# A planner's clock that lets GpSimd's masks and VectorE's SBUF operations exclude each other, in a two-layer transformer kernel

## The chip, the core and the metric

The kernel runs on one core of a Trainium2 chip. The metric is the device time of one launch in microseconds. The engines are named as in the profile: PE (TensorE matmul, with PEld its weight loads), DVE (VectorE), ACT (ScalarE), POOL (GpSimd) and SP (SyncE, which here only issues DMAs).

## The reference

Two blocks are applied twice in turn to x, 2048 rows of 512 in bfloat16, with the same weights both times:

```python
x = x + A(layernorm(x));  x = x + B(layernorm(x))      # and the same two lines again

# A: 32 heads of 16 columns, four segments of 512 rows each
logits = q @ k.T / 4 + mask;  a_dot = softmax(logits) @ v      # causal within its segment, as 0 / -1e9 by row and column
a_mem  = (phi(q) @ M) / (phi(q) @ z + 1e-6)                    # phi(t) = t + 1 if t > 0 else exp(t)
o      = g * a_mem + (1 - g) * a_dot                           # g = sigmoid(beta), one per head
M += phi(k).T @ v;  z += sum(phi(k))                           # carried from segment to segment
A      = o @ wo

# B
B      = (gelu(x @ w_gate) * (x @ w_up)) @ w_down              # 512 -> 1792 -> 512, tanh form of gelu
```

## The kernel before

The work goes by eight segments: four of the first pass and four of the second, numbered k = 0 to 7, each of 512 rows. For each there is an `Att` object (block A) and an `Ffn` object (block B). All weights, x and the segment's intermediates stay in SBUF. The eight PSUM banks of 128x512 float32 are handed out one by one (`pick`), and a bank is free again when some engine has read it.

PE's work comes in three tilings. A dense product of 128x128x512 is issued whole (line 532) or in four column pieces of 32 (line 527). The scores (line 992) run as four row tiles of 32 rows, and the product of probabilities and values, called flush (line 1008), as four column tiles. Between tilings PE switches.

For a segment's attention there are 36 rounds of scores. Two rounds fill two pairs of banks, ACT takes the exponential of each pair into a `pt` slot (line 1434), POOL or DVE zeroes the part above the diagonal (the masks, lines 1381, 1386 and 1391), and a flush uses nine rounds or so. DVE then transposes the flush's result (byq, line 1025), divides (ab, line 1033) and transposes back (aT, line 1040). Between the rounds stand the dense products: q, k, v; the memory's products; wo; 14 gate products, 14 up products and four down products of 14 steps. Their results are taken out of PSUM by DVE or ACT (`evict`, lines 517 and 518), and added to x by DVE (line 1081). Layer norm is on DVE (statistics at line 570, xn at line 600, sometimes on POOL). The normalised rows are turned by DMA transposes on SP's queue, or by PE and an eviction for those that `by_pe` names (line 642).

Gate results are kept in `gel_sb`. When all kept gates of a segment are there, `gelu_all` sets ACT to Gelu alone (`act.only`), which also loads another activation table, and ACT applies Gelu in place (line 1195). The last `direct` gates, by their number, stay in PSUM and get their Gelu straight from there (line 1121). Segment 7 takes all its Gelus straight from PSUM (line 1108).

No engine chooses anything when the kernel runs. The order of every engine's instructions is made when the kernel is built, by the function `order`. It keeps a clock for PE and one for each other engine (`Clocks`, `Engine`). At each step it asks what PE can do now: two rounds of scores (`rounds_now`), the next piece of an open product, or the product with the least due time among those that are ready by the clocks. If nothing is ready and a bank is free, it issues a fill, a matmul on the constant tile `warm`. If no bank is free it lets the clock run. Each other engine takes from its posted jobs the one with the least ready time plus slack (`Engine.serve`). The costs are numbers in the code, in microseconds. Due times and slacks are in `POLICY`, and `CHANGES` replaces some of them in single stretches of 20 us of the planned time. Only the order reaches the chip. Semaphores keep it right, and where a cost is wrong an engine waits.

VectorE's and GpSimd's operations with all operands in SBUF have a cost of type `Slowed`: a time alone and an amount that is added if the other engine's last such operation is still running by the clock:

```python
if isinstance(cost, Slowed):
    if self.rival.port > t + 0.1:
        t += cost.more
    self.port = t + cost
```

The mask operations of POOL have plain costs.

Of the kernel before, what the change touches and what calls it, by code (L numbers as in the profile page):

```python
# [11 lines left out]
ACT = mybir.ActivationFunctionType  # L12
# [16 lines left out]
FT = FF // P  # L29
# [18 lines left out]
def round_of(t):  # L48

    b, i = divmod(t, ROUNDS)  # L50
    if i == SHARED:
# [18 lines left out]
    flush_wait=31.032, piece_slack=12.114, kb_slack=17.26, mem_slack=-3.651, margin=2.436, qk_due=1.242,  # L70
    e_q=-0.78, e_k=1.726, exp_slack=-22.194, e_slack=6.379, phi_slack=16.481, gelu_slack=5.207, act_evict=5.099,
    first_evict=-1.454, gate_step=0.008, up_due=0.23, up_step=0.048, down_due=1.972, down_step=0.411,
    upd_due=0.836, kb_act=0.601, vz_slack=0.631, x_dve=1.439, v0_due=-1.871, x1_at=-24.71, x2_at=15.224,
    x3_at=27.505, x3_load=5.352, direct=2, gelu_tiles=1, look=3.643, lag=0.5, wv_at=6.266, xn_pool=3.14,
    kb_pool=4.2, cut_pool=2.678, at_pool=8.009, pe_turns=1, early=5.887, starve=0.39, near=-4.229, cap=3,
    soon=5.328)

CHANGES = {
    1: dict(flush_wait=32.067, phi_slack=16.21, gelu_slack=7.718, up_due=0.251, upd_due=0.421, x_dve=2.027,
        look=2.465, early=5.04),  # L80
    2: dict(flush_wait=32.067, phi_slack=16.21, gelu_slack=7.718, up_due=0.251, upd_due=0.471, x_dve=2.027,
        look=2.465, early=5.04),
    3: dict(flush_wait=29.115, piece_slack=3.287, kb_slack=20.041, mem_slack=-6.163, qk_due=1.326, e_q=-0.807,
        e_k=1.562, exp_slack=-23.374, phi_slack=17.368, gelu_slack=4.829, act_evict=3.476, first_evict=-1.146,
        up_due=0.102, up_step=0.03, down_due=1.953, down_step=0.413, upd_due=0.93, vz_slack=-1.163, look=4.182,
        xn_pool=4.557, kb_pool=4.735, cut_pool=0.095, at_pool=7.177, early=5.489, near=-2.667, cap=2, soon=4.536),
    4: dict(mem_slack=-5.18, margin=3.412, qk_due=1.158, exp_slack=-22.515, phi_slack=17.182, act_evict=5.723,
        down_due=2.119, vz_slack=0.498, look=3.219, xn_pool=4.585, cut_pool=3.546, at_pool=7.441, early=5.429,
        starve=0.478, soon=4.482),
    5: dict(kb_slack=15.09, mem_slack=-4.972, up_due=0.1, xn_pool=4.868, cut_pool=2.362),  # L90
    6: dict(mem_slack=-3.758, e_q=-0.911, e_k=1.815, act_evict=5.646, first_evict=-0.527, up_due=0.239,
        up_step=0.043, down_step=0.406, x_dve=1.274, direct=3, near=-5.575, cap=4),
    7: dict(flush_wait=27.914, mem_slack=-4.892, phi_slack=16.815, first_evict=-0.749, up_step=0.056, down_due=1.835,
        upd_due=0.824, kb_act=0.94, direct=1, lag=0.762, xn_pool=4.45, kb_pool=4.061, at_pool=7.125, early=5.542,
        starve=0.714, near=-4.302, cap=1, soon=3.714),
    9: dict(e_k=1.639, gelu_slack=5.187, up_due=0.23, up_step=0.05, kb_act=0.938, vz_slack=0.404, lag=0.612,
        kb_pool=3.937, cut_pool=3.32, early=5.784, cap=2, soon=5.439),
    10: dict(gelu_slack=5.187, up_due=0.23, upd_due=0.987, vz_slack=0.513, xn_pool=1.446, cut_pool=3.402,
        early=5.784, cap=2, soon=5.439),
    11: dict(gelu_slack=5.908, upd_due=0.987, vz_slack=0.513, xn_pool=1.446, cut_pool=3.402, early=5.784, cap=2,  # L100
        soon=5.439),
    12: dict(flush_wait=29.115, piece_slack=10.134, mem_slack=-4.176, margin=2.501, qk_due=1.047, e_k=1.581,
        e_slack=6.526, phi_slack=18.977, act_evict=5.661, first_evict=-0.966, gate_step=0.028, up_due=0.211,
        up_step=0.052, down_due=1.811, down_step=0.409, kb_act=3.137, x_dve=1.793, direct=1, look=2.233,
        cut_pool=2.844, early=5.595, cap=2, soon=4.119),
    13: dict(flush_wait=31.998, kb_slack=15.76, margin=2.188, qk_due=1.37, e_q=-0.681, e_k=1.607, exp_slack=-22.955,
        e_slack=8.005, phi_slack=17.246, gelu_slack=5.065, act_evict=6.326, first_evict=0.369, up_due=0.23,
        up_step=0.053, down_due=1.971, down_step=0.42, upd_due=0.833, kb_act=2.813, vz_slack=0.028, x_dve=1.225,
        direct=0, look=4.789, lag=0.833, xn_pool=1.003, kb_pool=6.227, cut_pool=1.872, early=4.965, starve=0.244,
        near=-4.281, soon=4.486),  # L110
    15: dict(flush_wait=29.717, piece_slack=13.149, kb_slack=19.294, mem_slack=-5.639, e_slack=6.767,
        first_evict=-0.318, up_due=0.26, up_step=0.056, down_due=2.016, kb_act=0.41, x_dve=1.289, look=2.582,
        cut_pool=4.981, at_pool=7.181, early=6.304),
    17: dict(flush_wait=30.781, piece_slack=8.881, kb_slack=18.357, mem_slack=-6.183, margin=2.678, qk_due=0.996,
        e_q=-0.614, e_k=1.779, exp_slack=-25.113, e_slack=8.371, phi_slack=17.054, gelu_slack=5.133, act_evict=5.437,
        gate_step=0.015, up_due=0.264, up_step=0.05, down_due=1.905, down_step=0.422, upd_due=0.6, kb_act=2.882,
        x_dve=2.377, gelu_tiles=3, look=2.018, lag=0.848, xn_pool=3.568, kb_pool=6.676, cut_pool=1.121,
        at_pool=7.491, early=5.072, near=-4.322, cap=5, soon=3.604),
    18: dict(flush_wait=34.707, piece_slack=8.536, kb_slack=18.053, mem_slack=-8.018, qk_due=1.188, e_q=-0.503,
        e_k=1.782, exp_slack=-23.593, e_slack=8.107, phi_slack=16.435, gelu_slack=5.168, act_evict=5.437,  # L120
        gate_step=0.007, up_step=0.045, down_due=2.315, upd_due=0.606, kb_act=1.877, vz_slack=-0.68, x_dve=1.741,
        gelu_tiles=2, look=2.51, lag=0.848, xn_pool=3.185, kb_pool=7.295, cut_pool=2.272, at_pool=6.929, early=5.072,
        near=-4.303, soon=3.604),
    20: dict(flush_wait=30.024, piece_slack=18.892, mem_slack=-5.208, qk_due=1.306, e_k=1.855, exp_slack=-24.126,
        e_slack=6.869, act_evict=6.671, first_evict=-1.8, gate_step=0.016, up_due=0.267, up_step=0.049,
        down_step=0.388, kb_act=1.799, vz_slack=-0.793, lag=1.151, kb_pool=3.298, cut_pool=2.948, at_pool=7.79,
        early=5.114, near=-5.599, soon=4.272),
    21: dict(flush_wait=28.52, piece_slack=18.892, mem_slack=-5.208, qk_due=1.306, e_q=-0.843, e_k=1.855,
        exp_slack=-24.126, e_slack=6.869, act_evict=6.671, first_evict=-1.8, gate_step=0.016, up_due=0.267,
        up_step=0.049, down_step=0.388, kb_act=1.799, vz_slack=-0.793, look=3.436, lag=1.151, kb_pool=3.298,  # L130
        cut_pool=2.948, at_pool=7.303, early=5.114, near=-5.599, soon=4.272),
    22: dict(flush_wait=30.024, piece_slack=18.892, mem_slack=-5.208, qk_due=1.306, e_q=-0.843, e_k=1.855,
        exp_slack=-24.126, e_slack=6.869, act_evict=6.671, first_evict=-1.8, gate_step=0.016, up_due=0.267,
        up_step=0.049, down_step=0.388, kb_act=1.799, vz_slack=-0.793, lag=1.151, kb_pool=3.298, cut_pool=2.948,
        at_pool=7.303, early=5.114, near=-5.599, soon=4.272),
    24: dict(kb_slack=19.342, mem_slack=-5.116, margin=2.033, e_slack=6.341, first_evict=-0.532, up_due=0.155,
        up_step=0.043, upd_due=0.729, vz_slack=0.073, look=4.821, lag=-0.099, at_pool=7.008),
    26: dict(kb_slack=19.342, mem_slack=-5.116, margin=2.033, e_slack=6.341, first_evict=-0.359, up_due=0.155,
        upd_due=0.729, kb_act=1.494, lag=-0.099, xn_pool=4.611, cut_pool=3.497, at_pool=7.008, cap=4),
    27: dict(kb_slack=19.342, mem_slack=-5.116, margin=2.033, e_slack=6.341, first_evict=-0.359, up_due=0.155,  # L140
        upd_due=0.729, kb_act=1.494, lag=-0.099, xn_pool=4.611, cut_pool=3.497, at_pool=7.008, cap=4),
}
WINDOW = 20.0


class Slowed(float):


    def __new__(cls, alone, more):
        self = super().__new__(cls, alone)  # L150
        self.more = more
        return self


class Engine:
# [4 lines left out]
    def __init__(self, overlap=0.0):  # L160
        self.free, self.overlap, self.jobs, self.table = 0.0, overlap, [], "exp"
        self.only, self.rival, self.port = None, None, 0.0
# [1399 lines left out]
```

## Time and profile before

| | us |
|---|---|
| median of 3 runs | 555.3 (553.71 to 556.18) |
| the profiled execution | 553.62 |
| its span, first to last instruction | 551.9 |
| PE busy | 536.3 (97%) |
| DVE busy | 463.3 (84%) |
| ACT busy | 428.2 (78%) |
| POOL busy | 304.2 (55%) |

In the profile a group of instructions is a line of the kernel, an engine, an operation, the tiles (out<-in), the shapes and a count. Behind the bar stand its busy time and the mean of one in nanoseconds, and behind the second bar the engine's idle time just before them and who ended it. A row of the timeline is a start, a length, an engine and a line, where like instructions that follow each other are merged into one row. Matmuls are pipelined, so one shows a longer time than the step from it to the next. A row of a stretch is its window and length, and PE's busy time with the number of instructions, its granted clock, and what DMA did. A row of the waits is who waited, for whom, microseconds in total, how many times, and the longest.

### The profile page before, as it was taken

The numbers are of one execution on the slowest core, as the hardware profiler recorded it, in microseconds if no ns is written. First come the engines' busy times: TensorE is split into PE (matmuls) and PEld (weight loads), VectorE is DVE, ScalarE is ACT, GpSimd is POOL, SyncE is SP. The second block draws the span as 40 slices with busy tenths as digits, with TensorE's granted clock in tenths as the row PEclk, the third lists the DMA queues.
The fourth block names the chain that finished last, engine by engine and source line by source line (L and its number), as shares of the span: only waits on it lengthen the run. The fifth ranks groups of instructions, "written<-read, shape, count | busy, mean of one in ns | idle before, by whom it ended". The sixth has DMA issues, their size and how long they took to land.

```text
span 551.9 us, 23372 instructions
## 1 busy us (share of the span) xinstructions
PE 536.3 (97%) x10286; PEld 279.5 (51%) x10286; DVE 463.3 (84%) x854; ACT 428.2 (78%) x557; POOL 304.2 (55%) x359
## 2 busy tenths in 40 slices
PE   7999999999999999999999989999999999999997
PEld 3454565554455454544554445554565556555544
DVE  6999999899998999879999897999779687876332
ACT  5899999987898978989899874898978977650330
POOL 2798889286763886336783372846867255200000
PEclk9999999999999999999999999999999999999999
DMA  8147401630140123310223031211222004100001
GB/s 248 42 96 194 140 20 24 163 47 7 32 78 12 23 41 61 59 23 3 40 40 61 2 42 23 50 34 31 51 51 51 2 13 89 23 2 21 20 1 38
DMA packets 67109, 27.59 MB, mean 50 GB/s; under 512 B 51392, under 2 KB 67008, under 8 KB 67008
## 3 DMA queue, kind: packets, MB, share of 16 engines
q1 hardware_dynamic: 66576, 25.84, 22.0%
q8 instruction: 80, 1.31, 1.0%
q10 hardware_dynamic: 432, 0.27, 0.2%
q14 instruction: 21, 0.17, 0.1%
HBM read 9.71 MB, written 2.10 MB: 21 GB/s over the span
## 4 chain that ended last, share of the span: by engine, by line
PE 73%; DVE 17%; issue 3%; ACT 2%; POOL 2%; DMA 2%; SPq 0%; DVEq 0%; ACTq 0%; POOLq 0%
PE ps L527 32%; PE ps L532 28%; PE ps L992 6%; PE ps L1008 5%; DVE st L570 2%; DVE x_sb L1081 2%; DVE xn L600 2%; DVE byq L1025 2%; ACT pt L1434 2%; DMA x_sb<-in_A_x_dram 2%; DVE phiq L799 1%; DVE kx L473 1%; DVE ab L1033 1%; POOL kx L473 1%; PE ps L642 1%
## 5 line engine op out<-in xcount | busy, mean ns | idle before, releaser
L1434 ACT ACTIVATE pt<-ps 128x1024 bf16<-128x1024 f32 x288 | 278.8, 1027 | 54.8 <-PE ps L992 47.3
L1381 POOL TENSOR_SCALAR_AFFINE_SELECT pt<-pt 128x256 bf16<-128x256 bf16 (+1 forms) x192 | 108.3, 579 | 102.9 <-ACT pt L1434 98.9
L1143 DVE TENSOR_TENSOR gel_sb<-gel_sb,ps 128x512 bf16<-128x512 bf16 x112 | 74.2, 683 | 28.4 <-PE ps L532 21.0
L1386 POOL TENSOR_SCALAR_AFFINE_SELECT pt<-pt 64x1024 bf16<-64x1024 bf16 x46 | 56.2, 1222 | 24.7 <-ACT pt L1434 20.0
L1081 DVE TENSOR_TENSOR x_sb<-x_sb,ps 128x512 bf16<-128x512 bf16 (+1 forms) x68 | 42.9, 645 | 26.6 <-PE ps L532 13.9
L527 PE MATMUL ps<-xnT,wu_sb 128*32 128x512 bf16 x1072 | 59.8, 379 | 0.0
L527 PE MATMUL ps<-wd_sb,gel_sb 128*32 128x512 bf16 (+1 forms) x1012 | 56.6, 367 | 0.2 <-DVE x_sb L1081 0.2
L818 POOL TENSOR_SCALAR e<-e 128x512 bf16<-128x512 bf16 x36 | 56.1, 1560 | 0.9
L527 PE MATMUL ps<-xnT,wg_sb 128*32 128x512 bf16 x924 | 55.6, 380 | 0.7 <-DVE gel_sb L517 0.6
L532 PE MATMUL ps<-xnT,wg_sb 128*128 128x512 bf16 x217 | 51.7, 380 | 0.3 <-DVE x_sb L1081 0.2
L532 PE MATMUL ps<-wd_sb,gel_sb 128*128 128x512 bf16 (+1 forms) x251 | 49.6, 345 | 0.8 <-DVE byq L1025 0.8
L1025 DVE STREAM_TRANSPOSE byq<-ps 128x512 f32<-128x512 f32 x64 | 44.5, 700 | 6.7 <-PE ps L1008 6.6
L1195 ACT ACTIVATE gel_sb<-gel_sb 128x512 bf16<-128x512 bf16 (+1 forms) x77 | 44.6, 668 | 0.1
L527 PEld LDWEIGHTS <-wu_sb 128*32 128x32 bf16 x1072 | 28.8, 97 | 27.1 <-issue 0.6
L532 PE MATMUL ps<-xnT,wu_sb 128*128 128x512 bf16 x180 | 41.7, 380 | 0.0
L570 DVE BATCH_NORM_STATS2 st<-x_sb 128x6 f32<-128x512 bf16 x60 | 40.6, 676 | 1.4 <-DMA x_sb<-in_A_x_dram 1.0
L517 DVE CAST gel_sb<-ps 128x512 bf16<-128x512 f32 x58 | 38.2, 679 | 2.9 <-PE ps L527 2.3
L527 PEld LDWEIGHTS <-gel_sb 128*32 128x32 bf16 x1012 | 25.6, 97 | 21.2 <-issue 1.8
L1008 PE MATMUL ps<-pt,vaug 128*32 128x256 bf16 (+2 forms) x1344 | 34.8, 238 | 0.0
L600 DVE TENSOR_SCALAR xn<-x_sb,mv,rs 128x512 bf16<-128x512 bf16 x57 | 32.8, 628 | 2.2 <-POOL rs L588 1.9
L527 PEld LDWEIGHTS <-wg_sb 128*32 128x32 bf16 x924 | 22.9, 97 | 21.3 <-issue 2.1
L532 PEld LDWEIGHTS <-gel_sb 128*128 128x128 bf16 x251 | 23.4, 98 | 19.7 <-issue 1.5
(146 smaller groups left out, 887.6 us busy)
## 6 DMA issues: line engine op xcount, KB each, us to landing
vz<-vaug SPq DMA_DIRECT2D x14, 136.0 KB, 2.6
wg_sb<-in_B_w_gate_dram SPq DMA_DIRECT2D x8, 224.0 KB, 4.4
wu_sb<-in_B_w_up_dram SPq DMA_DIRECT2D x8, 224.0 KB, 5.3
wd_sb<-in_B_w_down_dram SPq DMA_DIRECT2D x7, 256.0 KB, 5.5
x_sb<-in_A_x_dram SPq DMA_DIRECT2D x3, 512.0 KB, 7.6
out_dram<-x_sb SPq DMA_DIRECT2D x12, 128.0 KB, 1.8
xnT<-xn SPq DMA_TRANSPOSE x44, 2.5
wk_sb<-in_A_wk_dram SPq DMA_DIRECT2D x2, 256.0 KB, 6.5
```

What stands on the lines that cost most here:

```text
L527: nc.tensor.matmul(out[r], lhsT=lhsT[:, r], rhs=rhs, start=start, stop=stop, tile_position=(0, 32 * c))
L532: nc.tensor.matmul(out, lhsT=lhsT, rhs=rhs, start=start, stop=stop)
L570: nc.vector.bn_stats(out=self.st6[:, 0, :], in_=x_sb[:, self.tt0 + j, :])
L818: lambda eng: eng.tensor_scalar(out=e[0][:], in0=e[0][:], scalar1=1.0, scalar2=None, op0=ALU.min), summed)
L1008: nc.tensor.matmul(ps()[32 * j:32 * j + 32, q0:q0 + n], lhsT=va[:, ki * VW + g:ki * VW + g + 32], rhs=pt_all[:, places[i], j, c0:c0 + n], ...
L1025: nc.vector.transpose(out=self.byq[:, par, :, :].rearrange("p a c -> p (a c)"), in_=ps()[:])
L1081: ck.dve.post(ck.made(), slack, (0.15 + 0.00104 * (c1 - c0), lambda: nc.vector.tensor_tensor(out=xt, in0=xt, in1=ps()[:, 0:c1 - c0], op=AL ...
L1143: ck.dve.post(ck.made(), NORMAL, (0.683, lambda: nc.vector.tensor_tensor(out=g, in0=g, in1=ps()[:], op=ALU.mult), lambda t: (ps.read(t), e ...
L1195: return (0.205 + 0.427 * (f1 - f0), lambda: nc.scalar.activation(out=g, in_=g, func=ACT.Gelu_apprx_tanh), lambda t: self.gelu_done(t, f0, ...
L1381: nc.gpsimd.affine_select(out=view, in_=view, pattern=[[0, 4], [0, n], [1, C]], compare_op=ALU.is_ge, fill=0.0, base=C, channel_multiplier=-1)
L1386: nc.gpsimd.affine_select(out=view, in_=view, pattern=[[0, 4 * TPS], [1, C]], compare_op=ALU.is_ge, fill=0.0, base=0, channel_multiplier=-1)
L1434: nc.scalar.activation(out=pt_all[:, s0:s0 + 2, 2 * p:2 * p + 2, :].rearrange("p r h c -> p h r c"), in_=ps_all[:, pair[0]:pair[1] + 1, :] ...
```

## The change

The class `Slowed` becomes `Port`. A Port operation first waits, by the clock, until the other engine's hard Port operation ends, less 0.2 us. Operations of GpSimd on tensors with a scalar, and its addition to aT, are marked soft: they do not hold the other engine off, and the two cost 0.15 us if they meet. GpSimd's masks are hard Port operations now. Where a mask holds the port for more than 0.25 us longer, VectorE's Port jobs are put back by `shun` = 1.318 in the choice of the next job.

The Gelu stage is changed too. `direct` counts gates in the order in which they are done, not by number, and is 4 (2 before, and 0 to 3 in some stretches). Up to three neighbouring tiles go through one Gelu (one before, with few exceptions). The stage begins when no exponential is posted on ACT. While it lasts (`phase`) no new phi exponential starts, no new rounds of scores start while more than `hold` = 5 of the segment's 14 gates lack their Gelu, and the gates that are left are taken first.

The numbers of `POLICY` are new, `pe_turns` is 2 instead of 1 (the normalised rows of one more segment are turned by PE), and `CHANGES` is empty. The operations on data are the same in both kernels, but which engine does some of them, and the order on all engines, differ.

```diff
 POLICY = dict(
-    ..., x3_load=5.352, direct=2, gelu_tiles=1, look=3.643, ..., pe_turns=1, early=5.887, starve=0.39, ...)
+    ..., x3_load=17.807, direct=4, gelu_tiles=3, look=1.884, ..., pe_turns=2, gate_due=1.051, shun=1.318,
+    hold=5, early=5.58, starve=0.305, ...)
...
 CHANGES = {
-    1: dict(flush_wait=32.067, phi_slack=16.21, gelu_slack=7.718, up_due=0.251, upd_due=0.421, x_dve=2.027,
-        look=2.465, early=5.04),
...
 }
-class Slowed(float):
-    def __new__(cls, alone, more):
+class Port(float):
+    def __new__(cls, alone, soft=False):
         self = super().__new__(cls, alone)
-        self.more = more
+        self.soft = soft
         return self
...
-        job = min((j for j in jobs if j[0] + self.LATENCY <= start + 0.03), key=lambda j: j[0] + j[1])
+        held = self.rival is not None and self.rival.port > start + 0.25
+        job = min((j for j in jobs if j[0] + self.LATENCY <= start + 0.03), key=lambda j: j[0] + j[1] + (
+            self.shun if held and isinstance(j[2][0][0], Port) else 0.0))
...
-            if isinstance(cost, Slowed):
-                if self.rival.port > t + 0.1:
-                    t += cost.more
-                self.port = t + cost
+            if isinstance(cost, Port):
+                t += max(0.0, self.rival.port - t - 0.2)
+                if self.rival.soft > t + 0.1 or cost.soft and self.rival.port > t:
+                    t += 0.15
+                if cost.soft:
+                    self.soft = t + cost
+                else:
+                    self.port = t + cost
...
-            on_dve_or_pool(ready, self.slack, pol.xn_pool if self.key[0] == "xnTa" else None, Slowed(0.405, 0.22),
-                           Slowed(2.05, 0.1), lambda eng: made.append(self.normed(j, i, eng)), told)
+            on_dve_or_pool(ready, self.slack, pol.xn_pool if self.key[0] == "xnTa" else None, Port(0.405),
+                           Port(2.05, True), lambda eng: made.append(self.normed(j, i, eng)), told)
...
-                    steps += [(0.355, inverse, None), (Slowed(0.692, 0.15), scale, kept)]
+                    steps += [(0.355, inverse, None), (Port(0.692), scale, kept)]
...
-                    if ft < FT - self.direct:
+                    if self.n_gate <= FT - self.direct:
+                        self.kept.append(ft)
                         evict(ps, lambda: gel_sb[:, ft, :], lambda: ps()[:], told)
...
-                return Item(lambda: k + 1.2 + pol.gate_step * ft,
+                return Item(lambda: -0.8 if phase[0] == k else k + pol.gate_due + pol.gate_step * ft,
...
         def gelu_all(self, ready):
-            ck.act.only = "gelu"
-            ...
-            for f in range(0, kept, pol.gelu_tiles):
-                self.post_gelu(ready, gelu(f, min(f + pol.gelu_tiles, kept)), pol.gelu_slack)
-            for straight in self.straight:
-                self.post_gelu(*straight, URGENT)
+            phase[0], phase[1] = self.k, FT
+            def begin():
+                ck.act.only = "gelu"
+                t = max(ready, ck.pe)
+                ...
+                kept = sorted(self.kept)
+                while kept:
+                    n = 1
+                    while n < min(len(kept), pol.gelu_tiles) and kept[n] == kept[0] + n:
+                        n += 1
+                    self.post_gelu(t, gelu(kept[0], kept[0] + n), pol.gelu_slack)
+                    kept = kept[n:]
+                for straight in self.straight:
+                    self.post_gelu(*straight, URGENT)
+            ck.when(lambda: not any(j[3] == "exp" and not j[4] for j in ck.act.jobs), begin)
...
     def next_e():
-        if not e_slots.free or e_slots.queue:
+        if not e_slots.free or e_slots.queue or phase[0] is not None:
             return
...
     def rounds_now(idle=False):
-        if not streams or not rounds_ready(2):
+        if not streams or phase[0] is not None and phase[1] > pol.hold or not rounds_ready(2):
             return 0
...
-            ck.dve.post(at, pol.x_dve, (Slowed(0.9, 0.15), lambda: mask_both(slot), done.append), taken=taken)
-            ck.pool.post(at, NORMAL, (1.17, lambda: mask_half(slot, 0), None), (1.17, lambda: mask_half(slot, 1), done.append),
+            ck.dve.post(at, pol.x_dve, (Port(0.67), lambda: mask_both(slot), done.append), taken=taken)
+            ck.pool.post(at, NORMAL, (Port(1.14), lambda: mask_half(slot, 0), None), (Port(1.14), lambda: mask_half(slot, 1), done.append),
                          taken=taken)
         elif n:
-            ck.pool.post(at, NORMAL, (0.27 + 0.22 * n, lambda: mask(slot, n), done.append))
+            ck.pool.post(at, NORMAL, (Port(0.245 + 0.215 * n), lambda: mask(slot, n), done.append))
```

## The prediction

> **What bounds the kernel now.** I read the page first, for engine shares and the chain that ended last; then the stretches, for where TensorE (PE) idles; then PE's own waits, for what ends that idle time; then the timeline, for why what it waited for was late.
>
> ```profile
> PE 536.3 (97%) x10286; PEld 279.5 (51%) x10286; DVE 463.3 (84%) x854; ACT 428.2 (78%) x557; POOL 304.2 (55%) x359
> ...
> PE 73%; DVE 17%; issue 3%; ACT 2%; POOL 2%; DMA 2%; SPq 0%; DVEq 0%; ACTq 0%; POOLq 0%
> ```
>
> PE is the bound, and the chain is mostly PE following itself. So time can change in two ways only: more or less work in PE's stream, and more or less idle time between its pieces. The stretches place the idle time:
>
> ```profile
> 0.00:20.00 20.00, 16.26 (x122) 1.00 0.61 185
> 20.00:552.00 532.00, 520.09 (x10166) 1.00 0.22 45
> ```
>
> The clock is full in both. The first 20 us idle for 3.7 us: the start, written out by hand, which the change leaves alone. Behind it PE idles 532.0 - 520.1 = 11.9 us. Part of that is the end, where the last product's sum is added and stored:
>
> ```profile
> 548.73 0.42 DVE L1081 TENSOR_TENSOR x_sb<-x_sb,ps 128x256 bf16<-128x256 bf16 x1 [1.11 <-PE ps L532]
> ```
>
> PE is finished at 548.7, so 551.9 - 548.7 = 3.2 us belong to the end, and 11.9 - 3.2 = 8.7 us of idle time lie inside the body, where a new order can win or lose. PE's waits say for whom:
>
> ```profile
> PE ps L992 <- DVE byq L1025: 2.7, 2, 2.2
> PE ps L992 <- DVE x_sb L1081: 1.2, 2, 0.6
> PE ps L642 <- DVE xn L600: 1.1, 2, 0.6
> ...
> PE ps L532 <- DVE byq L1025: 0.8, 1, 0.8
> PE ps L992 <- ACT pt L1434: 0.7, 1, 0.7
> PE ps L527 <- DVE gel_sb L517: 0.6, 1, 0.6
> ...
> PE ps L527 <- DVE x_sb L1081: 0.2, 1, 0.2
> ...
> PE ps L532 <- DVE x_sb L1081: 0.2, 1, 0.2
> PE ps L992 <- DVE vaug L517: 0.2, 1, 0.2
> ```
>
> VectorE (DVE) ends 2.7 + 1.2 + 1.1 + 0.8 + 0.6 + 0.2 + 0.2 + 0.2 = 7.0 us of the 8.7, in 11 waits, nearly all for a PSUM bank that it reads too late. The longest, and the 0.8, in the timeline:
>
> ```profile
> 318.61 1.10 POOL L1381 TENSOR_SCALAR_AFFINE_SELECT pt<-pt 128x512 bf16<-128x512 bf16 x1 [0.26 <-ACT pt L1434]
> 319.11 3.10 DVE L600 TENSOR_SCALAR xn<-x_sb,mv,rs 128x512 bf16<-128x512 bf16 x3
> 319.68 2.38 POOL L1386 TENSOR_SCALAR_AFFINE_SELECT pt<-pt 64x1024 bf16<-64x1024 bf16 x2
> ...
> 325.58 0.70 DVE L1025 STREAM_TRANSPOSE byq<-ps 128x512 f32<-128x512 f32 x1
> 326.33 0.40 PE L992 MATMUL ps<-q,kf 16*128 16x256 bf16 x12 [2.19 <-DVE byq L1025]
> ```
> ```profile
> 196.91 0.40 DVE L600 TENSOR_SCALAR xn<-x_sb,mv,rs 128x512 bf16<-128x512 bf16 x1
> ...
> 198.46 1.14 POOL L1386 TENSOR_SCALAR_AFFINE_SELECT pt<-pt 64x1024 bf16<-64x1024 bf16 x1
> 198.58 1.24 PE L532 MATMUL ps<-wd_sb,gel_sb 128*128 128x512 bf16 x5 [0.78 <-DVE byq L1025]
> 198.95 1.18 DVE L1033 TENSOR_TENSOR ab<-byq,r 128x512 bf16<-128x512 f32 x1
> ```
>
> One xn takes DVE 0.40 us, and three beside GpSimd's (POOL's) masks take 3.10 instead of 1.2. An ab that starts 0.65 us before a mask ends (198.46 + 1.14 = 199.60) takes 1.18. GpSimd's other work does not hold it like that:
>
> ```profile
> 283.03 2.08 POOL L600 TENSOR_SCALAR xn<-x_sb,mv,rs 128x512 bf16<-128x512 bf16 x1
> ...
> 283.99 0.69 DVE L1033 TENSOR_TENSOR ab<-byq,r 128x512 bf16<-128x512 f32 x1
> ```
>
> Here ab runs inside a GpSimd xn and takes 0.69. So a mask cost the other ab 1.18 - 0.69 = 0.49 us, the rest of the mask less 0.16.
>
> **The planner's new clock.** The old clock adds a fixed 0.22 (xn) or 0.15 (ab) when the engines overlap. The new one makes a DVE operation marked Port wait until the mask's end less 0.2, and charges 0.15 against a GpSimd tensor_scalar. By the rows that is right: 0.65 - 0.2 = 0.45 against 0.49 measured, and about nothing for the second ab. The Trainium skill (SBUF, Who interferes with whom) states that whichever engine starts first takes the shared pair for its whole instruction and the other fully blocks; the mask row agrees within 0.16 us, the row at 283 does not. By that rule alone the second ab would have stood until 285.11, about 1.1 us longer, and the new soft price of 0.15 would be as wrong as the old clock; the sum does not use it.
>
> The clock itself executes nothing. What counts is the order it makes, and there I count, comparing the two programs' instructions.
>
> **PE's work.** Prices:
>
> ```profile
> 479.40 25.04 PE ps L527 x464
> ```
> ```profile
> 138.06 0.40 PE L642 MATMUL ps<-ident,xn 128*128 128x128 bf16 x4
> ...
> 320.82 1.03 PE L532 MATMUL ps<-xnT,wk_sb 128*128 128x512 bf16 x4
> 321.78 0.40 PE L992 MATMUL ps<-q,kx 32*128 32x256 bf16 x12
> ```
> ```profile
> L532 PE MATMUL ps<-wd_sb,gel_sb 128*128 128x512 bf16 x170 | 40.4, 380 | 0.8 <-DVE byq L1025 0.8
> ```
>
> A product in four column pieces takes 25.04 / (464/4) = 0.216 us. A whole one shows 0.380, pipelined: four take 1.03, a step of (1.03 - 0.38) / 3 = 0.217. So pieces or whole cost the same, and PE's 434 fewer instructions (9852 for 10286) are worth nothing. Behind the last of those four (started at 320.82 + 0.65 = 321.47) the score matmul starts at 321.78, 0.31 later: a change of tiling costs 0.31 - 0.216 = 0.095. A 128x128 transpose is (0.40 - 0.22) / 3 = 0.06, taking 0.22 as one's pipelined length. The counts:
> - Fill matmuls on the warm tile, issued where the planner finds nothing ready: 18 behind the start before (13 whole, 5 in pieces), 33 after (20 and 13). 15 x 0.216 = +3.2 us. They stand in the first two segments, as before.
> - pe_turns 2: segment 2's normalised rows are turned by PE too, 16 more transposes: +1.0. Four DMA transposes leave SP's queue (44 to 40), and with them their wait, which nothing on PE's list above shows, so I credit nothing; four more evictions of xnT (two on ACT, two on DVE) are in the counts below.
> - Changes of tiling: 301 for 293, +0.8.
>
> All else in PE's stream is equal. Sum: +5.0 us on the path, with no cover, since PE is the path.
>
> **The other engines.**
>
> ```profile
> L517 DVE CAST gel_sb<-ps 128x512 bf16<-128x512 f32 x58 | 38.2, 679 | 2.9 <-PE ps L527 2.3 <-PE ps L532 0.2
> L1195 ACT ACTIVATE gel_sb<-gel_sb 128x512 bf16<-128x512 bf16 x73 | 38.9, 624 | 0.0
> L1195 ACT ACTIVATE gel_sb<-gel_sb 128x1536 bf16<-128x1536 bf16 x4 | 5.7, 1482 | 0.0
> L1121 ACT ACTIVATE gel_sb<-ps 128x512 bf16<-128x512 f32 x13 | 6.9, 588 | 0.0
> L473 DVE TENSOR_SCALAR kx<-kf,masks 128x512 bf16<-128x512 bf16 x22 | 10.9, 507 | 0.4
> L1434 ACT ACT_TABLE_LOAD x6 | 7.7, 1283 | 0.1
> ```
>
> DVE loses 16 gate evictions (10.9 us), 9 net of q, kf, vaug and xnT (about 6) and 14 masked copies (14 x 0.507 = 7.1), and gains some 3 in e and aT: near -21 us of 463. ACT gains 15 Gelus from PSUM (15 x 0.588 = 8.8), and about 14 us of evictions and copies, and saves in grouped Gelus 44.6 - (7 x 0.624 + 21 x 1.482) = 9.1: near +14 of 428. GpSimd: 4 more mask halves, 6 more masked copies, 7 fewer e, 3 fewer aT: about nothing. All this is beside PE and costs nothing while PE has ready work; it matters since DVE, the engine PE waits for, gets slack, and ACT at 78% + 3% still has more than PE.
>
> Unknown is how much of the 7.0 us of DVE waits goes. A wait also hides the tail of the matmul ahead of it, which counts as busy (0.380 - 0.216 = 0.164), so 11 waits cost 7.0 + 1.8 = 8.8. Bounds: none goes (0), or all idle time of the body goes, 8.7 + 1.8 = -10.5; new waits could also come (below, rival two). I take -8.8: the rows at 198 and 319 show these waits made by masks that the old clock priced too low and the new one prices rightly, and DVE has 21 us less to do. ACT's 0.7 and the small rest stay; those are late next.
>
> **Sum.** 551.9 + 5.0 - 8.8 = 548.1 span. The profiled execution took 553.62, so 1.7 lie around its span: 549.8. It stands 1.7 under the median of the three runs (555.3), which gives 551.5.
>
> **Rivals.**
> - *The waits stay.* This is the change not doing what it says. For it: the mean xn on DVE is 0.628 by its group (row below), and the old clock's 0.405 + 0.22 = 0.625 was right on average; only the spread was wrong, and a late DVE may come from any drift. Then only the added work is left: 551.9 + 5.0 + 3.4 = 560.3, slower. It decides from the point where fewer than 5.0 of the 8.8 go. Against it: both longest waits sit behind masks.
> - *The Gelu pause.* No score round starts now while more than five of a segment's gates lack Gelu. Seven segments pause. The first up product needs the table load and a group of three: 1.28 + 1.48 = 2.8 us, against 1.28 + 0.62 = 1.9. In this time PE has the direct gates, 4 x 4 x 0.216 = 3.5 us, a margin of 0.7 us. If ACT is late by one more group of 1.48, each pause costs 0.8 and 7 give 5.6: 551.5 + 5.6 = 557.1, and to 562 if the DVE waits stay in part. It turns the verdict from 0.5 us per pause. For it: ACT is busier; against it: ACT already idles for scores.
> - *All idle goes.* -10.5 instead of -8.8, and the fills stand where PE would have waited anyway for transposes (0 instead of 3.2): 551.5 - 1.7 - 3.2 = 546.6. For it: PE idles 2.3 us in the short stretch where most fills stand, 120 to 142; against it: that idle is partly in the 7.0 already.
>
> ```profile
> L600 DVE TENSOR_SCALAR xn<-x_sb,mv,rs 128x512 bf16<-128x512 bf16 x57 | 32.8, 628 | 2.2 <-POOL rs L588 1.9 <-POOL rs L1231 0.2
> ```
> ```profile
> 120.00:142.00 22.00, 19.66 (x417) 1.00 0.07 15
> ```
> ```profile
> ACT pt L1434 <- PE ps L992: 47.3, 64, 8.6
> ```
>
> **How the numbers follow.** Half a per cent, 2.8 us, is about what can be told from no change: faster ends at 552.5, slower begins at 558.1. The forecast 0.42, all idle goes 0.15, the waits stay 0.25, the pause 0.18. The forecast's own range is 548 to 555 (two thirds to all of what can go), so about 0.12 of its 0.42 falls within half a per cent, as does about 0.07 of the pause's. Faster 0.46, same 0.20, slower 0.34. Both signs hold chance, so the range reaches from 546 (all idle goes) to 561 (the waits stay).
>
> **What would show it.** Right: PE's waits for byq, x_sb and xn under 2 us together behind the start; PE's body idle near 2 us; 33 fills behind the start; DVE near 442 us busy, ACT near 442; ab, xn and phiq on DVE nearer their lone times, since the planner steers them clear of masks. Wrong: waits for DVE that keep their total (the first rival), or waits of up matmuls for gel_sb on ACT at the seven Gelu stages (the second).

## The result and the profile after

The changed kernel takes 548.8 us (median of 6 runs, 548.19 to 550.25), beside 555.5 for the kernel before (553.3 to 556.18). The ratio is 0.989, with a 95% interval of 0.9866 to 0.9913: faster by 1.1%. The profiled execution took 549.09, with a span of 547.4 (before: 551.9). The prediction said 551.5 and a span of 548.1.

Of the 6.7 us between the medians some 4.5 lie in the order, and the rest seems to come from PE's clock, which most executions of the kernel before did not keep full (last section).

The page of the kernel after shows the engine shares and the chain, as before. Its line numbers are those of the changed kernel: 470 and 475 are the products in pieces and whole (527 and 532 before), 936 the scores (992), 952 the flush (1008), 969 byq (1025), 743 phi (799).

```profile
PE 533.9 (98%) x9794; PEld 277.9 (51%) x9852; DVE 444.8 (81%) x823; ACT 435.9 (80%) x545; POOL 307.4 (56%) x359
...
PE 85%; DVE 9%; issue 2%; DMA 2%; ACT 2%; POOL 0%; SPq 0%; DVEq 0%; POOLq 0%; ACTq 0%
```

The chain that ended last has less of VectorE in it (9% for 17%) and more of PE. PE's waits show where that went:

```profile
PE ps L475 <- issue: 4.9, 31, 0.2
PE ps L349 <- DVE warm L340: 1.1, 1, 1.1
PE ps L936 <- ACT pt L1394: 0.7, 1, 0.7
PE ps L475 <- DVE byq L969: 0.7, 1, 0.7
PE ps L470 <- issue: 0.3, 1, 0.3
PE ps L595 <- DVE xn L543: 0.3, 1, 0.3
```

The waits for VectorE that made 7.0 us of the body are down to one of 0.7 (`warm` and line 595 are the start). The rows put down to "issue" are not waits. The trace holds 9794 of the program's 9852 matmuls but all 9852 weight loads; where the record of a whole product is missing, a hole of 0.16 us is left, or one of 0.05 us, which is too short for this list. The stretch behind the start shows them too:

```profile
20.00:548.00 528.00, 516.75 (x9674) 1.00 0.23 44
```

Up to 547.4 that is 10.7 us of idle time. The last sum is added at 544.28, so 3.1 belong to the end. Some 6 are missing records: nearly all of the 5.2 in the rows above, and 1.2 in 23 of the shorter holes. About 1.5 us of real idle time are left in the body, where there were 8.7.

VectorE now waits for PE where PE waited for VectorE. The first row is of before, the second of after, from the list of all engines' waits:

```profile
DVE byq L1025 <- PE ps L1008: 6.6, 7, 3.0
```
```profile
DVE byq L969 <- PE ps L952: 18.9, 19, 3.5
```

**The measure for the experiments.** Another order has other work in it, so I split each span in two. The first part is PE's stream: every matmul of the program's order at its own step, the median time from its start to the next start in the trace of before (216 ns for 512 columns, about 96 more at a change of tiling). The rest, less 9.5 us, is the idle of the body. The 9.5 are the start (the first matmul at 1.1 us, and 4.9 above the steps in the first 20 us) and the end (the last matmul begins 3.5 before the end). This measure doesn't depend on which records are missing. It is larger than the page's idle time (8.7 and about 1.5), since it also counts the tails of matmuls ahead of a wait, and every step that is longer than its median.

| | stream | of it fills | idle of the body | fills + idle |
|---|---|---|---|---|
| before | 526.9 | 18 = 3.9 us | 551.9 - 526.9 - 9.5 = 15.5 | 19.4 |
| after | 532.0 | 33 = 7.1 us | 547.4 - 532.0 - 9.5 = 5.9 | 13.0 |

The gain in span, 4.5 us, is 9.6 less idle time for 5.1 more in the stream. Each row is one execution, and so is each run below unless it says otherwise. The recorded spans of before reach from 551.9 to 555.2 and those of the changed kernel from 546.5 to 548.5, so a difference of 2 us in idle time tells little, and one of 8 tells much.

### The profile page after: what moved, and what is told of

Same layout as the page of the kernel before. It is cut to its first block, busy times and chain, and to the rows that moved or that the text cites. A ratio compares the mean times of both kernels' runs of the same rounds, so it can differ in the third digit from the quotient of the medians.

```text
span 547.4 us, 22326 instructions
## 1 busy us (share of the span) xinstructions
PE 533.9 (98%) x9794; PEld 277.9 (51%) x9852; DVE 444.8 (81%) x823; ACT 435.9 (80%) x545; POOL 307.4 (56%) x359
## 4 chain that ended last, share of the span: by engine, by line
PE 85%; DVE 9%; issue 2%; DMA 2%; ACT 2%; POOL 0%; SPq 0%; DVEq 0%; POOLq 0%; ACTq 0%
PE ps L475 41%; PE ps L470 30%; PE ps L936 7%; PE ps L952 6%; DMA x_sb<-in_A_x_dram 2%; DVE st L513 2%; ACT pt L1394 1%; DVE x_sb L1025 1%; DVE byq L969 1%; DVE xn L543 1%; PE ps L585 1%; DVE phiq L743 1%; PE ps L583 1%; DVE vaug L460 0%; DVE kf L460 0%
## 5 line engine op out<-in xcount | busy, mean ns | idle before, releaser
L475 PE MATMUL ps<-xnT,wg_sb 128*128 128x512 bf16 x266 | 63.6, 380 | 1.2 <-issue 0.8
L475 PE MATMUL ps<-xnT,wu_sb 128*128 128x512 bf16 x265 | 62.2, 380 | 1.5 <-issue 1.1
L762 POOL TENSOR_SCALAR e<-e 128x512 bf16<-128x512 bf16 x29 | 46.0, 1587 | 1.1
L475 PEld LDWEIGHTS <-wu_sb 128*128 128x128 bf16 x278 | 25.9, 98 | 31.2 <-issue 1.1
L470 PE MATMUL ps<-xnT,wg_sb 128*32 128x512 bf16 x676 | 41.2, 380 | 0.0
L475 PEld LDWEIGHTS <-wg_sb 128*128 128x128 bf16 x279 | 25.8, 98 | 29.7 <-issue 0.6
L470 PE MATMUL ps<-xnT,wu_sb 128*32 128x512 bf16 x680 | 38.6, 379 | 0.0
L416 POOL TENSOR_SCALAR kx<-kf,masks 128x512 bf16<-128x512 bf16 x22 | 35.0, 1592 | 2.0 <-ACT kf L461 0.8
L1149 ACT ACTIVATE gel_sb<-gel_sb 128x1536 bf16<-128x1536 bf16 (+1 forms) x28 | 33.5, 1283 | 0.0
L543 DVE TENSOR_SCALAR xn<-x_sb,mv,rs 128x512 bf16<-128x512 bf16 x57 | 28.0, 538 | 6.3 <-POOL rs L531 4.0
```

What stands on the lines that cost most here:

```text
L470: nc.tensor.matmul(out[r], lhsT=lhsT[:, r], rhs=rhs, start=start, stop=stop, tile_position=(0, 32 * c))
L475: nc.tensor.matmul(out, lhsT=lhsT, rhs=rhs, start=start, stop=stop)
L762: lambda eng: eng.tensor_scalar(out=e[0][:], in0=e[0][:], scalar1=1.0, scalar2=None, op0=ALU.min), summed)
```

## The experiments

My theory: PE waited because the old planner's clock priced GpSimd's masks wrongly against VectorE. In its code a mask is a plain cost and never sets `port`, so a VectorE operation beside a mask was planned at its lone time. Its rivals: that VectorE's lighter load, the new Gelu stage, or the one lucky set of numbers took the waits away.

**The old clock alone put back.** The changed kernel, with `Slowed` and the old costs, and without `shun`:

```diff
-            if isinstance(cost, Port):
-                t += max(0.0, self.rival.port - t - 0.2)
-                ...
+            if isinstance(cost, Slowed):
+                if self.rival.port > t + 0.1:
+                    t += cost.more
+                self.port = t + cost
```

> The changed kernel with the old clock alone (fixed additions where the engines overlap, masks at plain cost, no shun); Gelu stage and policy numbers stay the new ones. PE's own stream, each matmul at its step, is 526.9 us before, 532.0 after and 541.6 here (80 fill matmuls behind the start for 18 and 33). Span = that sum + 9.5 for start and end + idle of PE in the body; by that measure the idle is 15.5 before and 5.9 after. If the clock is what took the waits for VectorE away, the idle comes back to about 15.5: span 566. If it was VectorE's lighter load, the Gelu stage or the policy numbers, it stays near 6: span 557.

Measured: span 564.7, so idle 564.7 - 541.6 - 9.5 = 13.6. PE waits for VectorE again; the first rows of its waits:

```profile
PE ps L946 <- DVE byq L963: 1.6, 1, 1.6
PE ps L464 <- DVE kf L454: 1.4, 1, 1.4
...
PE ps L930 <- DVE vaug L454: 0.7, 2, 0.5
PE ps L930 <- DVE gel_sb L1084: 0.6, 1, 0.6
```

**The new clock alone put in.** The kernel before, with `Port` and the new costs (no `shun`), and its own policy and stretches.

> The kernel before with the new clock alone (mask and SBUF operations exclude each other in planning); Gelu stage, policy and windows stay the old ones. PE's own stream is 540.4 us (78 fills). If the clock removes the waits, the idle of PE's body falls from 15.5 to about 6: span 556. If the waits come from VectorE's load or from the policy, it stays near 15: span 565.

Measured: span 557.4, idle 7.5. No wait for VectorE in the body is over 0.6 us:

```profile
PE ps L536 <- ACT pt L1438: 1.5, 4, 0.9
...
PE ps L646 <- DVE xn L604: 0.6, 1, 0.6
PE ps L536 <- DVE gel_sb L1147: 0.5, 1, 0.5
```

So the planner's clock decides the idle, both ways. VectorE's lighter load is not needed for it: VectorE is busy 457.4 us here, 5.9 less than before, where the changed kernel has 18.5 less. But this kernel is slower than before (559.1 us against 555.7 for one execution of each): its order has 78 fills, 16.8 us. The clock alone did not make the kernel faster. Numbers that were chosen under the old clock give a worse order under the new one.

**The masks left out, orders kept.** In both kernels, GpSimd's masks are planned as ever but not issued:

```diff
     def mask(slot, n):
         ...
-        nc.gpsimd.affine_select(out=view, in_=view, pattern=[[0, 4], [0, n], [1, C]], ...)
+        pass
```

and likewise in `mask_half`.

> The kernel before in its own order, with GpSimd's masks above the diagonal left out (what lies above the diagonal in those rounds is not zeroed; VectorE's few masks stay). If masks holding VectorE cause the waits, byq, x_sb, xn and gel_sb are read in time: idle of PE's body falls from 15.5 to 7 or less, span about 543, VectorE's xn near 0.42 us and ab near 0.69. If VectorE is late for another reason, idle stays within 2 us of 15.5 and the span near 550.

> The changed kernel in its own order, with GpSimd's masks left out in the same way. If the new order has the masks' hold planned in, PE gains little: idle of the body 4 to 6 for 5.9, span 545.5 to 547.5. If the masks still cost PE time, the span falls by 4 us or more, as before does without them.

Measured: before without masks 542.6, idle 6.2 for 15.5; after without masks 545.4, idle 3.9 for 5.9. VectorE's groups in the first of these, where xn was 628 ns and phiq 774:

```profile
L600 DVE TENSOR_SCALAR xn<-x_sb,mv,rs 128x512 bf16<-128x512 bf16 x57 | 22.9, 456 | 0.7 <-POOL rs L588 0.5 <-POOL rs L1231 0.2
L1033 DVE TENSOR_TENSOR ab<-byq,r 128x512 bf16<-128x512 f32 x32 | 22.2, 692 | 1.1
L799 DVE SCALAR_TENSOR_TENSOR phiq<-q,e 128x512 bf16<-128x512 bf16 x24 | 16.8, 699 | 0.1
```

The masks cost the old order 9.3 us and the new one 2.0, no more than executions of one kernel differ by. Leaving them out also frees GpSimd's own queue, so this pair alone doesn't show that the hold of VectorE is the whole of it. No wait of PE before, though, was for a mask or for anything of GpSimd's.

**The same in a second old-clock order.** The kernel with the old clock from above, masks left out.

> The changed kernel planned with the old clock, as in the run of the old clock alone (span 564.7, stream 541.6, idle 13.6), with GpSimd's masks left out of the program in that same order. If masks holding VectorE are what the old clock gets wrong, the idle falls to 6 or less: span 557 or less. If the old clock is wrong elsewhere too, most of the 13.6 stays: span over 561.

Measured: span 555.9, idle 4.8 for 13.6. Two old-clock orders, with 18 and with 80 fills, each lose some 9 us of idle time when the masks go.

**The Gelu stage, the pause, shun and the numbers.** Four kernels with the new clock, each with another part undone or moved. The first sets `direct=2, gelu_tiles=1`.

> The changed kernel with direct = 2 and gelu_tiles = 1, as the policy before had them; clock and all other numbers new. The order that comes out has 80 fills, and PE's own stream is 541.9. If the clock alone decides how long PE waits, the idle of its body is 5 to 8 as in the changed kernel (5.9): span 541.9 + 9.5 + 6.5 = 558. If the new Gelu stage is what took the waits away, the idle goes back towards 15: span 566.

The second lets scores and phi go on in the Gelu stage:

```diff
-        if not e_slots.free or e_slots.queue or phase[0] is not None:
+        if not e_slots.free or e_slots.queue:
...
-    hold=5, ...
+    hold=14, ...
```

> The changed kernel without the pause in the Gelu stage: new rounds of scores and phi exponentials may start at any time; clock and numbers new. PE's own stream is 542.9 (83 fills). If the pause has no part in PE's waits, the idle is 5 to 8: span 559. If it is the pause that keeps PE from waiting for Gelu, the idle is 10 or more: span 562.5 or more. If the pause costs, the idle is under 4: span under 556.

The third sets `shun=0.0`.

> The changed kernel with shun = 0: in planning VectorE's operations still wait for a mask's end, but are not put back in the choice of the next job. PE's own stream is 543.7 (87 fills). If pricing the hold is what keeps the waits short, the idle is 5 to 8: span 559.5. If putting VectorE's operations back does it, the idle is 10 or more: span 563 or more.

The fourth multiplies every fractional number of the policy by 1 plus a random amount with a spread of 3% (such as `flush_wait=22.690` for 22.067).

> The changed kernel with every number of its policy moved at random by some 3% (counts of things stay). PE's own stream is 537.1 (56 fills). If the new clock alone keeps PE's waits short, whatever the numbers, the idle of the body is about 6 as in the changed kernel: span 537.1 + 9.5 + 6 = 552.6. If the 5.9 belongs to the one selected set of numbers, the idle is 10 or more: span 556.6 or more.

| new clock, changed | span | stream | fills | idle |
|---|---|---|---|---|
| Gelu as before | 556.4 | 541.9 | 80 | 5.0 |
| no pause | 560.0 | 542.9 | 83 | 7.6 |
| no shun | 557.4 | 543.7 | 87 | 4.2 |
| numbers moved by 3% | 554.0 | 537.1 | 56 | 7.4 |

In all four the idle stays between 4 and 8. None of these parts took the waits away. All four spans are 6.6 to 12.6 us longer than the changed kernel's, and what they lose is mostly fills: the selected numbers had 33, any step away 56 to 87. So what a part is worth by itself can't be read from these totals; a step off a selected order costs more than the part.

Idle time alone also flatters the new clock, for a planner that foresees a wait can put a fill there. Fills and idle together are 22.3, 25.5, 23.0 and 19.5 us in these four, and 24.3 in the kernel before with the new clock alone; the kernel before has 19.4. Only the selected numbers of the changed kernel get below that, to 13.0 with the new clock, and they have 30.9 with the old one. In these runs the gain stands only where the new clock and the selected numbers meet.

**The stretches of before left out.** The kernel before with `CHANGES` empty.

> The kernel before with its single policy in all stretches (CHANGES empty), old clock. PE's own stream is 528.0 (21 fills for 18). If the idle follows the clock, it is about 15 as before: span 552.5. If it was the set of changed stretches that tuned the waits away or brought them, the idle moves by 3 us or more either way.

Measured: span 551.3, idle 13.8. It is the third old-clock order, and it idles like the others. The span is no longer without the stretches than with them (551.9).

**The fills left out.** The changed kernel in its own order, without the 33 fill matmuls:

```diff
-                product(ps(), warm[:], wide)
+                product(ps(), warm[:], wide, issued=False)
```

> The changed kernel in its own order, with the 33 fill matmuls behind the start left out (they compute nothing that is used). PE's own stream falls from 532.0 to 524.8. If the fills are work on the path with nothing behind them to wait for, as the prediction's +3.2 for 15 of them has it, the span falls by their 7.1 us, to 540.3. If PE would stand idle there in any case until its next product is ready, the span stays within 1 us of 547.4 and the idle of the body rises by up to 7.

Measured: 550.4 us (median of 4), 0.9913 of before with an interval of 0.9888 to 0.9939, so not faster than the changed kernel at 0.989. The profiled span is 546.8: 0.6 less for 7.1 us of work left out, which is less than executions differ by, and the idle is 12.5. PE stands idle where the fills stood; and the clock granted to it halves. All four executions have a mean granted clock of 0.996 or 0.997, all six of the changed kernel 1.00. Three stretches of this kernel (window, length, PE's busy time and instructions, its granted clock, DMA), and then two of the changed kernel that cover the same time:

```profile
71.00:74.40 3.40, 3.40 (x48) 1.00 0.20 38
74.40:77.80 3.40, 1.96 (x76) 1.00 0.02 5
77.80:81.20 3.40, 3.25 (x62) 0.50 0.00 0
```
```profile
70.00:77.80 7.80, 7.75 (x136) 1.00 0.09 19
77.80:81.20 3.40, 3.40 (x91) 1.00 0.02 5
```

Half of the clock for 3.4 us is up to 1.7 us of PE's time, by estimate. So of the 7.1 us some 4.9 come back as waits, up to 1.7 as the slower clock, and 0.6 are gained.

## Why the prediction was right, and where not

- *PE is the bound, and its idle in the body is VectorE's lateness.* Right: 7.0 us of waits for VectorE, and 0.7 after.
- *The old planner's clock made that lateness, by its price for masks.* Right, and the best supported point: three old-clock orders idle 13.6 to 15.5, six new-clock orders 4.2 to 7.6 (the changed kernel's 5.9 among them), and without masks 4.8 and 6.2 for two of the old-clock ones. But the prediction misread the price. It has a fixed 0.22 for xn and 0.15 for ab wherever the engines overlap; by the code that is added only beside GpSimd's other work, and beside a mask nothing is. That 0.405 + 0.22 = 0.625 met the measured mean of xn, 0.628, was a coincidence and no support for the first rival.
- *-8.8 for the waits.* Measured: -9.6 of idle. By the page's rows it is 7.0 to 0.7 with the tails of 11 waits and one: 8.8 to 0.9, -7.9. The size was right.
- *+3.2 for fills, "on the path, with no cover".* This step failed in its reasoning, not in the sum. Fills do have a cover: the wait that would stand in their place. Left out, they give back 0.6 of 7.1, or at most some 2.3 but for the slower clock. The sum came out all the same. The likely reason, which no run separates, is that of the idle that went some 3 us became fills: the sum has them once as gain, in the 8.8, and once as cost, and the two cancel. What the change gained is in fills and idle together, 19.4 to 13.0, or 6.4; the prediction's two terms make 8.8 - 3.2 = 5.6.
- *+1.0 for transposes and +0.8 for changes of tiling.* 6.4 - 4.5 = 1.9 is what remains for them. Neither was tried alone.
- *Span 548.1, median 551.5.* The span was 547.4. That closeness is in part luck: the span it starts from, 551.9, is the shortest of ten recorded for before. Of the 2.7 us by which the median came lower, 0.7 lie in the span. The other 2.0 are the step from the profiled execution to the median: before, the median stood 1.7 above the execution, and I carried that over; after, it stands 0.3 below (548.8 and 549.09). The term was taken for a constant. The recorded clocks say what it likely is: the profiled execution of before was one of two in ten with the full clock, and half the clock for 3.4 us would make up to 1.7 us (an estimate).
- *What would show it.* VectorE was to be near 442 us (444.8), ACT near 442 (435.9, so about half of the 14 us that were expected), the body's idle near 2 (about 1.5), 33 fills (they are there). Wrong was that VectorE's operations would come nearer their lone times since the planner steers them clear of masks. xn did (628 to 538 ns) and ab (740 to 712), but phiq and e got slower (774 and 793 before):

```profile
L743 DVE SCALAR_TENSOR_TENSOR phiq<-q,e 128x512 bf16<-128x512 bf16 x24 | 22.4, 944 | 0.0
L743 DVE SCALAR_TENSOR_TENSOR e<-kf,e 128x512 bf16<-128x512 bf16 x20 | 17.8, 894 | 0.0
```

For these the new order doesn't avoid the hold, it allows for it. In the timeline of after, phiq meets a mask, takes 1.64, and PE goes on:

```profile
350.36 2.34 POOL L1346 TENSOR_SCALAR_AFFINE_SELECT pt<-pt 64x1024 bf16<-64x1024 bf16 x2
...
351.61 1.64 DVE L743 SCALAR_TENSOR_TENSOR phiq<-q,e 128x512 bf16<-128x512 bf16 x1
351.76 0.40 PE L936 MATMUL ps<-q,kx 32*128 32x256 bf16 x12
...
352.09 1.70 PE L470 MATMUL ps<-xnT,wg_sb 128*32 128x512 bf16 x28
```

- *The rivals.* The waits did not stay. The pause does not make PE wait: PE's list of after has no wait for a Gelu, and without the pause the idle is 7.6, no less than with it. That all idle would go was too much, but its claim that the fills stand where PE would have waited anyway was right.

What stays open: how much the Gelu stage and `shun` are worth in a set of numbers selected for them. No order was selected here without them, and none under the old clock with the new Gelu stage. Nor was the masks' price changed alone: the two runs that exchange the clock exchange all of its costs, and only the runs without masks point at the masks.

## What to carry to other kernels

Where two engines lock each other out, price it as a wait for the other's end, and see that every operation that holds the lock is priced at all. Here the masks cost time on their own engine alone, and leaving them out of the program gave the bounding engine 9 us. A mean that agrees (0.625 and 0.628) does not test a price: an order that is written down beforehand has to be right at each place. When a planned order is compared, split the span into the bounding engine's stream and its idle: a better cost model shows in the idle, and a changed number in the stream. Then look at fills and idle together, as one can stand for the other. Don't judge one part of a searched order by the total after taking it out, since any step from the selected numbers cost 6.6 us or more here.

## What the runs showed of the hardware that was not expected

The clock granted to PE halved for 3.4 us without any long pause. In the stretch before, PE was busy 1.96 of 3.40 us, in short pieces; its waits there were these, in the timeline of the kernel without fills:

```profile
75.68 0.20 PE L937 MATMUL ps<-q,kf 16*128 16x64 bf16 x2 [0.43 <-ACT pt L1395]
76.12 0.40 PE L937 MATMUL ps<-q,kf 16*128 16x64 bf16 x10 [0.23 <-DVE byq L970]
...
77.95 0.37 PE L953 MATMUL ps<-pt,vaug 128*32 128x64 bf16 x5 [0.84 <-POOL pt L1342]
```

The longest is 0.84 us, and it ends in the slow stretch. The Trainium skill (TensorE: Matmul & The Clock Gate, HAM oscillation) gives as the rule that there be no gap of PE over about 3.4 us. The length of the slow stretch agrees with that window; the rule for when it comes does not, since no gap here is longer than 0.84 us. A large share of idle time in such a window is not the rule either. In the kernel before, at the wait of 2.19 us, PE was busy less than in the 1.96 us above, and the clock stayed full:

```profile
324.70:328.10 3.40, 1.77 (x19) 1.00 0.23 41
```

What decides it stays open. With the fills, which compute nothing, the clock stayed full in all six executions of the changed kernel.

The kernel before did not keep it. Its profiled execution did, but of nine others whose clock was recorded eight had a mean granted clock of 0.996 or 0.997 and spans of 553.5 to 555.2, and one had 1.000 and 552.4. A mean of 0.997 is what the one slow stretch leaves in the kernel without fills. No execution of before with the lower clock was traced, so where it fell is not shown.

GpSimd's masks hold VectorE to their end, less 0.16 us in the row at 198 of before, but its operations of a tensor with a scalar do not: ab ran in 0.69 us inside a GpSimd xn of 2.08. Close behind the start of one, though, VectorE loses more than the 0.15 us of the new model: in the kernel before, ab took 0.38 us longer than 0.69. And the addition to aT, which the model calls soft, held phiq as a mask does in the changed kernel, to its end less 0.15 us (122.09 + 1.64 - 0.70 = 123.03, against 122.02 + 1.16 = 123.18):

```profile
86.77 1.48 POOL L818 TENSOR_SCALAR e<-e 128x512 bf16<-128x512 bf16 x1
86.85 1.07 DVE L1033 TENSOR_TENSOR ab<-byq,r 128x512 bf16<-128x512 f32 x1
```
```profile
122.02 1.16 POOL L987 TENSOR_TENSOR aT<-aT,amT 128x512 bf16<-128x512 bf16 x1
122.09 1.64 DVE L743 SCALAR_TENSOR_TENSOR phiq<-q,e 128x512 bf16<-128x512 bf16 x1
```

So the split into hard and soft fits the masks, and the soft part only in the main; six orders planned with it idled 4.2 to 7.6 us.
